# A block-sparse attention and a bilinear layer on one core: the second chunk's first-layer products are no longer parked in DRAM, and follow those of the first chunk

## The chip, the cores and the metric

One core of a Trainium2 chip. The metric is the device time of one execution in microseconds (us), lower is better. PE is the matrix engine, DVE the vector engine, ACT the scalar engine, POOL GpSimd, SP the engine whose queue issues most DMAs; ACT issues some too. PEld is PE's weight load.

## The reference, cut to what matters

```python
B, H, S, D = 4, 8, 768, 64                      # block of 32 positions, 24 blocks
scores = scale * q @ k^T                         # 768 x 768 for each of 32 heads
mask   = |blk_i - blk_j| <= 1, or first/last block row or column,
         or one of 3 sampled blocks of this query block
attn   = softmax(where(mask, scores, -1e9)) @ v
x      = attn.transpose(0, 2, 1, 3).reshape(3072, 512)
out    = ((x @ w_a) * (x @ w_b)) @ w_out         # 512 -> 1536 -> 512, fp32
```

## The kernel before

Work is cut into 12 **chunks** of 256 positions (3 in each of 4 batches) and each chunk into 8 **units**, one block of 32 query positions over all 8 heads; unit number n counts in the order of the work, so chunk 0 is units 0 to 7, chunk 1 units 8 to 15, chunk 2 units 16 to 23. Units whose block is the first or last of a batch are dense (units 8, 23, 24, ...), the others gather 8 key blocks.

*Attention of a unit* (`attend`, `attend_quad`): scores `s` on PE, row minimum `low` on DVE, exponentials `sm` on ACT (L898, L990), both 16-bit halves `hl` on ACT or DVE (L790, L793, L797), a transposing DMA `pt<-hl` on SP's queue (L920, L1015), and products `av` with the gathered values `VG` on PE (L816). Two units share one `av` tile; `output_half` writes its two halves as `xT` (L1060, L1063), the input of the layer. `s` has 2 buffers, `sm`, `hl` and `pt` 3 each. In `values` ACT also reads each block of raw values from `stage` (`va`, L515); the loads that fill `stage` are issued from ACT's own queue (L472, L507).

*The layer of a chunk cc* is 12 pieces f of 128 columns. First products `ab` (L1098, 24 matmuls): x times piece f of `w_a` and `w_b`; 2 buffers. `inner` makes the product `a` on ACT and DVE (L1126, L1129; 3 buffers of tag "a"), `split` its two parts `gh` (ACT, L1153) and `gl` (DVE, L1156; 2 buffers each). Second products `o` (L1184 to L1186, 6 matmuls): both parts times piece f of `w_out`, summed over f in two PSUM banks, which the next chunk may use when `store` has copied them (L1199, L1200). The weights come in and are prepared on the run while chunk 0 is worked on.

What is special in this kernel is **chunk 1**. Its first products stand in a flow of their own beside those of chunk 0 and wait for the same weights (`w_ready[f]`). Its products `a` are not split: `inner` writes each to DRAM (`parked_g`, L1134, 128 KB), and when the second products of chunk 1 begin, `unpark` reads them back as `u` (L1147) and splits these. Chunk 2's first products wait until all of it is split (`split_done`).

The order of all instructions is made when the kernel is built. Every piece of work is a flow (a Python generator) that asks for an engine; `Plan.run` gives the engine to the request that could start first by the planner's estimates, weighed with a rank (units have the lowest, `R_P2` second products, `R_P1` first products). Within an engine the program then runs in just this order: what waits holds up what stands behind it. This goes for SP's and ACT's DMA queues too.

Of the kernel before, what the change touches and what calls it, by code (L numbers as in the profile page):

```python
# [11 lines left out]
F32 = mybir.dt.float32  # L12
# [23 lines left out]
A_BUFS = 3  # L36
# [16 lines left out]
LEAD_K, LEAD_V, LEAD_Q, LEAD_X, LEAD_G = 10, 9, 8, -1, 2  # L53
GATE_KV, GATE_Q, GATE_G = 10, 5, 4
R_W, R_W_STEP = 8, 0.2
PARK = True
W_PE, W_DVE, W_ACT, W_POOL, W_SP = 0, 1, 0, 0, 2
SLACK = 0
R_NOW, R_P2, R_P1 = -50, 8000, 9000
# [179 lines left out]
def sp(ns, moved, fn):  # L239
    return [Way("SP", ns, fn, moved)]  # L240
# [3 lines left out]
def kernel(  # L244
# [40 lines left out]
    def take(tag, bufs):  # L285
        return rings.setdefault(tag, Ring(bufs)).take()
# [782 lines left out]
            read.fire(left.at + LATE_AV)  # L1069


    parked_g = dram.tile([NF, P, CH], F32, name="parked_g")
    g_parked = [Event() for _ in range(NF)]
    split_done = [Event() for _ in range(NF)]
    ready = {(cc, f): Event() for cc in range(NC) for f in range(NF)}
    parts = {}
    f1_ready = {(b, f): Event() for b in range(B) for f in range(NF)}

    def first_products(ccs):
        for cc in ccs:  # L1080
            b, c = chunks[cc]
            xc = xT[cc % 2]
            yield x_ready[cc]
            if cc == 2 and PARK:
                yield split_done[NF - 1]
            if cc == 0:
                plan.start(second_products(), R_P2)
            for f in range(NF):
                if cc < 2 and (cc == 0 or PARK):
                    yield w_ready[f]  # L1090
                read = yield from take("ab", 2)
                ab = psum.tile([P, 2, CH], F32, tag="ab", name=f"ab{cc}_{f}", bufs=2)

                def products(f=f):
                    for i in range(2):
                        for kt in range(KT):
                            for part, a in ((0, 0), (1, 0), (0, 1)):
                                mm(  # L1098
                                    ab[:, i, :], wab[:, f, i, part, kt, :], xc[:, kt, a, :],
                                    start=(i == 0 and kt == 0 and part + a == 0),  # L1100
                                    stop=(kt == KT - 1 and a == 1),
                                    skip_group_check=True,
                                )

                t = yield pe(2680, products)
                if f == NF - 1:
                    ffn_done[cc].fire(t)
                plan.start(inner(cc, f, ab, read), R_NOW, t)

    def inner(cc, f, ab, read):  # L1110
        b, c = chunks[cc]
        fb = f1[b % 2]
        fs = slice(0, NF) if b > 0 else slice(f, f + 1)
        rb = rscale[:, at_v + b : at_v + b + 1]
        if cc % NCH == 0 and (b == 0 or f == 0):
            pair = rscale[:, at_w + 2 * fs.start : at_w + 2 * fs.stop]
            pair = pair.rearrange("p (f i) -> p f i", i=2)
            t = yield dve(220, lambda: nc.vector.scalar_tensor_tensor(
                fb[:, fs], pair[:, :, 0], rb, pair[:, :, 1], ALU.mult, ALU.mult
            ))  # L1120
            f1_ready[b, f].fire(t)
        else:
            yield f1_ready[b, f if b == 0 else 0]
        e_a = yield from take("a", A_BUFS)
        a_sb = work.tile([P, CH], F32, tag="a", name=f"a{cc}_{f}", bufs=A_BUFS)
        yield act(470, lambda: nc.scalar.activation(  # L1126
            a_sb, ab[:, 0, :], AF.Copy, scale=fb[:, f : f + 1]
        ))
        t = yield dve(420, lambda: nc.vector.scalar_tensor_tensor(  # L1129
            a_sb, a_sb, rb, ab[:, 1, :], ALU.mult, ALU.mult  # L1130
        ))
        read.fire(t)
        if cc == 1 and PARK:
            t = yield sp(650, 364, lambda: nc.sync.dma_start(parked_g[f], a_sb))  # L1134
            e_a.fire(t)
            g_parked[f].fire(t)
            return
        yield from split(cc, f, a_sb, e_a)

    def unpark():  # L1140
        for f in range(NF):
            yield g_parked[f]
            if f >= 2:
                yield split_done[f - 2]
            e_a = yield from take("a", A_BUFS)
            a_sb = work.tile([P, CH], F32, tag="a", name=f"u{f}", bufs=A_BUFS)
            t = yield sp(650, 364, lambda f=f: nc.sync.dma_start(a_sb, parked_g[f]))  # L1147
            plan.start(split(1, f, a_sb, e_a), R_NOW, t)

    def split(cc, f, a_sb, e_a):  # L1150
        e_h = yield from take("gh", 2)
# [5 lines left out]
        e_a.fire(t)  # L1157
        parts[cc, f] = (gh, gl, e_h, e_l)
        ready[cc, f].fire(t + LATE_G)
        if cc == 1 and PARK:  # L1160
            split_done[f].fire(t)

    def second_products():
        banks, o_read = [None] * NJ, [None] * NJ
        for cc in range(NC):
            b, c = chunks[cc]
            if cc == 1 and PARK:
                plan.start(unpark(), R_NOW)
            rows = out[b * S + c * CH : b * S + (c + 1) * CH, :].rearrange(
                "(j p) d -> j p d", j=NJ  # L1170
            )
# [35 lines left out]
    with tc.manual_schedule():  # L1207
# [8 lines left out]
        plan.start(gather_keys(0), -LEAD_G)  # L1216
        plan.start(gather_values(0), -LEAD_G)
        plan.start(attend(*units[0]), 0)
        if PARK:
            plan.start(first_products([0, *range(2, NC)]), R_P1)  # L1220
            plan.start(first_products([1]), R_P1 + 1)
        else:
            plan.start(first_products(range(NC)), R_P1)
        plan.run()


# [64 lines left out]
```

## Time and profile before

| what | value |
|---|---|
| device time, median of 3 runs (range) | 901.85 us (900.5 to 905.66) |
| the profiled execution: its own time / its span | 901.24 us / 899.5 us |
| busy in the span: PE, PEld, DVE, ACT, POOL | 86%, 69%, 64%, 52%, 20% |

The span is what the profiler saw between the first and the last instruction; 1.7 us lie around it. A busy share is a mean over the whole span. "Granted clock" is the TensorE clock as a share of its full 2.4 GHz; 0.5 is its other level, 1.2 GHz.

### The profile page before, as it was taken

The numbers are of one execution on the slowest core, as the hardware profiler recorded it, in microseconds if no ns is written. First come the engines' busy times: TensorE is split into PE (matmuls) and PEld (weight loads), VectorE is DVE, ScalarE is ACT, GpSimd is POOL, SyncE is SP. The second block draws the span as 40 slices with busy tenths as digits, with TensorE's granted clock in tenths as the row PEclk, the third lists the DMA queues.
The fourth block names the chain that finished last, engine by engine and source line by source line (L and its number), as shares of the span: only waits on it lengthen the run. The fifth ranks groups of instructions, "written<-read, shape, count | busy, mean of one in ns | idle before, by whom it ended". The sixth has DMA issues, their size and how long they took to land.

```text
span 899.5 us, 23840 instructions
## 1 busy us (share of the span) xinstructions
PE 770.2 (86%) x9024; PEld 619.3 (69%) x9024; DVE 580.0 (64%) x1533; ACT 464.3 (52%) x1118; POOL 176.9 (20%) x416
## 2 busy tenths in 40 slices
PE   0132499678989999999999899999998999999998
PEld 0022277557768777777777678788776878888886
DVE  3898999986558677665677577645867736342222
ACT  4675576586446566754456468335536424232222
POOL 0652142322003332110132331001322200000000
PEclk9998599899999999999999999999999999999999
DMA  9978999979878699985867999637766516351000
GB/s 228 287 186 218 243 235 252 222 193 206 215 205 181 140 194 210 198 181 136 173 155 170 180 211 206 153 82 159 180 134 155 125 29 153 80 121 27 25 1 24
DMA packets 212221, 145.50 MB, mean 162 GB/s; under 512 B 152841, under 2 KB 180490, under 8 KB 211338
## 3 DMA queue, kind: packets, MB, share of 16 engines
q1 hardware_dynamic: 201280, 106.22, 54.3%
q10 hardware_dynamic: 10826, 37.76, 14.4%
q8 instruction: 71, 1.16, 0.5%
q14 instruction: 44, 0.36, 0.1%
HBM read 87.82 MB, written 14.16 MB: 113 GB/s over the span
## 4 chain that ended last, share of the span: by engine, by line
PE 55%; DMA 14%; DVE 10%; ACT 7%; issue 2%; SPq 2%; ACTq 0%; POOL 0%
PE ab L1098 30%; PE o L1184 6%; PE av L816 5%; DMA pt<-hl 5%; PE o L1186 5%; PE o L1185 5%; DMA q<-in_q_dram 3%; PE s L772 3%; DVE low L888 1%; DVE hl L797 1%; DVE xT L1063 1%; DMA VG<-vd 1%; DVE QT L649 1%; DMA u<-parked_g 1%; ACT sm L898 1%
## 5 line engine op out<-in xcount | busy, mean ns | idle before, releaser
L1098 PE MATMUL ab<-xT,wab 128*128 128x256 f16 x3456 | 404.7, 274 | 12.7 <-ACT xT L1060 6.9
L1098 PEld LDWEIGHTS <-wab 128*128 128x128 f16 x3456 | 329.7, 98 | 78.5 <-issue 37.7
L1129 DVE SCALAR_TENSOR_TENSOR a<-a,rscale,ab 128x256 f32<-128x256 f32 x144 | 68.6, 478 | 112.1 <-ACT a L1126 110.9
L1184 PE MATMUL o<-woh,gh 128*128 128x512 f32 x288 | 127.1, 441 | 6.8 <-ACT gh L1153 6.4
L1126 ACT ACTIVATE a<-ab,f 128x256 f32<-128x256 f32 x144 | 67.5, 468 | 120.3 <-PE ab L1098 114.4
L898 ACT ACTIVATE sm<-s,low,cq 128x256 f32<-128x256 f32 x176 | 97.9, 559 | 58.7 <-DVE low L891 29.4
L816 PE MATMUL av<-pt,VG 128*128 128x64 f16 x2688 | 103.2, 196 | 28.9 <-DMA pt<-hl 14.9
L816 PEld LDWEIGHTS <-VG 128*128 128x128 f16 x2688 | 94.6, 100 | 48.1 <-issue 35.5
L573 POOL COPY KG<-keysT 128x384 int32<-128x384 int32 x88 | 56.9, 647 | 356.5 <-PE s L772 325.9
L797 DVE SCALAR_TENSOR_TENSOR hl<-sm,den,hl 128x256 f16<-128x256 f32 (+1 forms) x208 | 104.3, 510 | 21.4 <-ACT hl L790 18.6
L1186 PE MATMUL o<-woh,gl 128*128 128x512 f32 x288 | 115.2, 400 | 0.5 <-DVE gl L1156 0.5
L1185 PE MATMUL o<-wol,gh 128*128 128x512 f32 x288 | 113.6, 395 | 0.0
L578 POOL COPY KG<-keysT 128x128 int32 x264 | 94.5, 394 | 42.9 <-POOL KG L573 23.2
L1153 ACT CAST gh<-a 128x256 fp32r<-128x256 f32 x132 | 53.1, 403 | 59.2 <-DVE a L1129 58.0
L1156 DVE TENSOR_TENSOR gl<-a,gh 128x256 fp32r<-128x256 f32 x132 | 58.2, 441 | 32.3 <-ACT gh L1153 31.6
L1184 PEld LDWEIGHTS o<-woh,gh 128*128 128x128 f32 x288 | 54.7, 190 | 27.7 <-ACT gh L1153 10.0
L772 PE MATMUL s<-KG,QT 128*32 128x256 f16 x1408 | 58.8, 291 | 16.8 <-DMA QT<-QT 16.6
L873 PE MATMUL s<-mrows,ident 128*32 128x192 bf16 (+1 forms) x352 | 25.6, 280 | 54.7 <-ACT sm L898 27.8
L1063 DVE SCALAR_TENSOR_TENSOR xT<-av,xT 64x256 f16<-64x256 f32 x96 | 40.4, 421 | 44.3 <-ACT xT L1060 43.4
L1186 PEld LDWEIGHTS o<-woh,gl 128*128 128x128 f32 x288 | 54.6, 189 | 16.6 <-DVE gl L1156 4.3
L888 DVE TENSOR_REDUCE low<-s 128x2 f32<-128x512 f32 x88 | 59.9, 682 | 6.4 <-PE s L772 6.1
L772 PEld LDWEIGHTS <-QT 128*32 128x32 f16 x1664 | 43.7, 101 | 29.5 <-issue 24.1
(92 smaller groups left out, 736.0 us busy)
## 6 DMA issues: line engine op xcount, KB each, us to landing
VG<-vd SPq DMA_DIRECT2D x284, 64.0 KB, 2.2
VG<-vd SPq DMA_DIRECT2D x88, 192.0 KB, 3.3
VG<-vd SPq DMA_DIRECT2D x32, 384.0 KB, 3.8
q<-in_q_dram ACTq DMA_DIRECT2D x12, 512.0 KB, 6.0
QT<-QT SPq DMA_DIRECT2D x24, 256.0 KB, 3.8
vd<-vs SPq DMA_DIRECT2D x16, 384.0 KB, 4.1
out_dram<-ou SPq DMA_DIRECT2D x24, 256.0 KB, 2.4
stage<-in_k_dram ACTq DMA_DIRECT2D x12, 384.0 KB, 4.2
```

The costliest lines, as they stand in the source:

```text
L578: nc.gpsimd.tensor_copy(to[:, :, (5 + r) * w : (6 + r) * w], of[:, :, bass.ds(at, w)])
L772: mm(to[h * BLK : (h + 1) * BLK], q_block(cc, i, 4 * hq + h, a), rhs(4 * hq + h), start=(first and a == 0), stop=(a == 1), skip_group_chec ...
L797: t = yield dve(221 + n * 1.03, lambda: nc.vector.scalar_tensor_tensor(lo, sm, over, hi, ALU.mult, ALU.subtract))
L816: mm(av[:, g, i % 2, :], w, pt[:, y, cols], start=(i % 2 == 0 and g == 0 and first and n + m == 0), stop=(last and n == len(terms) - 1 and ...
L888: yield dve(685, lambda: nc.vector.tensor_reduce(mx, ps, axis=mybir.AxisListType.X, op=ALU.max, negate=True))
L898: t = yield act(750, lambda hq=hq: nc.scalar.activation(sm[:, hq], ps[:, hq], AF.Exp, bias=low[:, at, hq, 0:1], scale=cq[:, cc, hq : hq + ...
L1098: mm(ab[:, i, :], wab[:, f, i, part, kt, :], xc[:, kt, a, :], start=(i == 0 and kt == 0 and part + a == 0), stop=(kt == KT - 1 and a == 1) ...
L1126: yield act(470, lambda: nc.scalar.activation(a_sb, ab[:, 0, :], AF.Copy, scale=fb[:, f : f + 1]))
L1129: t = yield dve(420, lambda: nc.vector.scalar_tensor_tensor(a_sb, a_sb, rb, ab[:, 1, :], ALU.mult, ALU.mult))
L1184: mm(po, gh[:, js], woh[:, f, :], start=(f == 0), stop=False)
L1185: mm(po, gh[:, js], wol[:, f, :], start=False, stop=False)
L1186: mm(po, gl[:, js], woh[:, f, :], start=False, stop=(f == NF - 1))
```

## The change

Chunk 1 is treated like all others: its first products wait in one flow behind those of chunk 0, its products are split as they are made, and `parked_g`, `unpark`, `split_done` and the 24 transfers are gone.

```diff
-    def first_products(ccs):
-        for cc in ccs:
+    def first_products():
+        for cc in range(NC):
             b, c = chunks[cc]
             xc = xT[cc % 2]
             yield x_ready[cc]
-            if cc == 2 and PARK:
-                yield split_done[NF - 1]
             if cc == 0:
                 plan.start(second_products(), R_P2)
             for f in range(NF):
-                if cc < 2 and (cc == 0 or PARK):
+                if cc == 0:
                     yield w_ready[f]
...
         read.fire(t)
-        if cc == 1 and PARK:
-            t = yield sp(650, 364, lambda: nc.sync.dma_start(parked_g[f], a_sb))
-            e_a.fire(t)
-            g_parked[f].fire(t)
-            return
         yield from split(cc, f, a_sb, e_a)
-
-    def unpark():
-        for f in range(NF):
-            yield g_parked[f]
-            if f >= 2:
-                yield split_done[f - 2]
-            e_a = yield from take("a", A_BUFS)
-            a_sb = work.tile([P, CH], F32, tag="a", name=f"u{f}", bufs=A_BUFS)
-            t = yield sp(650, 364, lambda f=f: nc.sync.dma_start(a_sb, parked_g[f]))
-            plan.start(split(1, f, a_sb, e_a), R_NOW, t)
...
         for cc in range(NC):
             b, c = chunks[cc]
-            if cc == 1 and PARK:
-                plan.start(unpark(), R_NOW)
...
-        if PARK:
-            plan.start(first_products([0, *range(2, NC)]), R_P1)
-            plan.start(first_products([1]), R_P1 + 1)
-        else:
-            plan.start(first_products(range(NC)), R_P1)
+        plan.start(first_products(), R_P1)
         plan.run()
```

Since the planner makes the order anew, instructions move. Ahead of the places shown here, which the trace before reaches at 202 us (SP, and ACT and DVE with the split of f = 0) and 207.69 us (PE), the order is the same on every engine. Line numbers of the changed kernel are 1 lower up to L1060 and 6 to 25 lower in the layer.

SP's queue, from the transposing load of the third block of keys of batch 1 (`keysT1<-ks1_2`) on: `pt17` and `pt18` are the transposed rows of units 17 and 18, `ou0_0` and `ou0_1` the output of chunk 0. Before:

```order
L496 DMA_TRANSPOSE keysT1_78<-ks1_2_2571 128x12x128
L1134 DMA parked_g_103<-a1_0_2720 128x256
L1134 DMA parked_g_103<-a1_1_2784 128x256
L673 DMA QT3_2468<-QT3_2468 64x2048 x2
L920 DMA_TRANSPOSE pt17_2566<-hl17_2515 128x8x128
L1147 DMA u0_2852<-parked_g_103 128x256
L1203 DMA out_0_dram<-ou0_0_2849 128x512
L1203 DMA out_0_dram<-ou0_1_2850 128x512
L1134 DMA parked_g_103<-a1_2_2884 128x256
L496 DMA_TRANSPOSE keysT1_78<-ks1_3_2679 128x12x128
L1147 DMA u1_2927<-parked_g_103 128x256
L920 DMA_TRANSPOSE pt18_2814<-hl18_2756 128x8x128
```

The same place of SP's queue in the changed kernel:

```order
L495 DMA_TRANSPOSE keysT1_78<-ks1_2_2570 128x12x128
L672 DMA QT3_2467<-QT3_2467 64x2048 x2
L919 DMA_TRANSPOSE pt17_2565<-hl17_2514 128x8x128
L1178 DMA out_0_dram<-ou0_0_2848 128x512
L1178 DMA out_0_dram<-ou0_1_2849 128x512
L919 DMA_TRANSPOSE pt18_2815<-hl18_2755 128x8x128
L495 DMA_TRANSPOSE keysT1_78<-ks1_3_2678 128x12x128
L919 DMA_TRANSPOSE pt19_2839<-hl19_2785 128x8x128
```

Two parkings no longer stand ahead of `pt17`, and `pt18` comes right behind the output stores, ahead of the last block of keys.

ACT, from the product `a1_2` (chunk 1, f = 2) on: `sm21` and `sm22` are exponentials of units 21 and 22, `va1_3` the reading of a raw value block of batch 1. Before:

```order
L1126 ACTIVATE a1_2_2884<-ab1_2_2804,f1_0_97 128x256
L898 ACTIVATE sm21_2887,den_96<-s21_2753,low_95,cq_94 128x256
L898 ACTIVATE sm22_2959,den_96<-s22_2889,low_95,cq_94 128x256 x2
L515 ACTIVATE va1_3_2901,bound_v_90<-stage_76 128x768
L1153 CAST gh1_0_2926<-u0_2852 128x256
L1126 ACTIVATE a1_3_3004<-ab1_3_2885,f1_0_97 128x256
```

The same place of ACT in the changed kernel:

```order
L1120 ACTIVATE a1_2_2887<-ab1_2_2804,f1_0_97 128x256
L897 ACTIVATE sm21_2862,den_96<-s21_2752,low_95,cq_94 128x256 x2
L506 DMA stage_76<-in_v_dram 128x768
L897 ACTIVATE sm22_2945,den_96<-s22_2860,low_95,cq_94 128x256
L1132 CAST gh1_2_2937<-a1_2_2887 128x256
L897 ACTIVATE sm22_2945,den_96<-s22_2860,low_95,cq_94 128x256
L514 ACTIVATE va1_3_2943,bound_v_90<-stage_76 128x768
L1120 ACTIVATE a1_3_2989<-ab1_3_2888,f1_0_97 128x256
L1059 ACTIVATE xT0_87<-av0_16_2549 64x4x64 x2
L1132 CAST gh1_3_3038<-a1_3_2989 128x256
```

The load that fills the buffer which `va1_3` reads is now issued behind both exponentials of unit 21 (before, it stood ahead of `a1_2`), and the split of f = 0 to 2 stands ahead of `va1_3` where before the first one, of `u0`, stood behind it.

On PE the same rows stand at this place in another order. Before, behind the scores of unit 22: `ab1_3`, `ab1_4`, `av` of unit 17, scores of unit 23, and only then `o` of f = 0. In the changed kernel: `o` of f = 0 and 1, `ab1_3`, `av` of unit 17, the first half of the scores of unit 23, `av` of unit 18, the second half, `o` of f = 2 and 3, `ab1_4`. Further on, before, `ab2_0` (the first product of chunk 2) follows the last `av` of unit 23 directly; in the changed kernel the scores of unit 27 and an `av` of unit 24 stand between, and `o` of f = 11 comes behind `ab2_0`. PE's order is the same in both again from the eleventh first product of chunk 6 on.

## Rows read from the trace of the kernel before

**Rows 1.** The page: busy us of the engines (share of the span) and instructions, and PE's busy tenths in 40 equal slices of the span (22.5 us each).
```profile
PE 770.2 (86%) x9024; PEld 619.3 (69%) x9024; DVE 580.0 (64%) x1533; ACT 464.3 (52%) x1118; POOL 176.9 (20%) x416
...
PE   0132499678989999999999899999998999999998
```

**Rows 2.** Busy time by stage: from us : to us, length, busy us (instructions) of PE, PEld, DVE, ACT, POOL, granted clock, share of the DMA engines' time, GB/s.
```profile
211.00:272.00 61.00, 54.50 (x604) 42.43 (x601) 35.08 (x90) 28.79 (x71) 7.62 (x21) 0.97 0.83 206
272.00:580.00 308.00, 296.02 (x3734) 238.10 (x3733) 214.80 (x595) 180.94 (x443) 73.10 (x192) 1.00 0.83 179
580.00:900.00 320.00, 309.96 (x3307) 253.35 (x3303) 152.33 (x400) 118.76 (x298) 30.68 (x82) 1.00 0.40 93
```

**Rows 3.** PE's waits between 272 and 580 us, the three largest of seven groups: instruction waited <- what ended the wait: us in all, times, longest.
```profile
PE av L816 <- DMA pt<-hl: 3.4, 2, 2.6
PE s L873 <- ACT sm L898: 3.3, 4, 1.3
PE o L1184 <- ACT gh L1153: 3.2, 5, 1.4
```

**Rows 4.** PE in order of time, the rows with a wait between 207 and 272 us, and the row where the order begins to differ: start, us, what, [idle before <- what ended it].
```profile
207.69 5.42 PE L1098 MATMUL ab<-xT,wab 128*128 128x256 f16 x48
215.05 0.88 PE L816 MATMUL av<-pt,VG 128*128 128x64 f16 x24 [1.95 <-DMA pt<-hl]
218.77 2.78 PE L1098 MATMUL ab<-xT,wab 128*128 128x256 f16 x24 [0.44 <-DVE a L1129]
259.27 0.69 PE L816 MATMUL av<-pt,VG 128*128 128x64 f16 x18 [0.22 <-DMA pt<-hl]
262.35 0.79 PE L1184 MATMUL o<-woh,gh 128*128 128x512 f32 x1 [2.39 <-ACT gh L1153]
268.75 0.38 PE L1098 MATMUL ab<-xT,wab 128*128 128x256 f16 x2 [0.85 <-ACT xT L1060]
269.65 2.56 PE L1098 MATMUL ab<-xT,wab 128*128 128x256 f16 x22 [0.52 <-DVE xT L1063]
```

**Rows 5.** PE in order of time, pieces of work that follow each other without a wait at full clock; the distance of two starts is what a piece takes.
```profile
241.57 0.47 PE L1184 MATMUL o<-woh,gh 128*128 128x512 f32 x1
...
243.04 2.79 PE L1098 MATMUL ab<-xT,wab 128*128 128x256 f16 x24
245.67 0.86 PE L816 MATMUL av<-pt,VG 128*128 128x64 f16 x24
246.47 0.51 PE L772 MATMUL s<-keysT,QT 128*32 128x384 f16 x8
246.91 0.87 PE L816 MATMUL av<-pt,VG 128*128 128x64 f16 x24
```

**Rows 6.** The granted clock in the 2 us in which the wait until 262.35 ends (columns as in rows 2), and PE's rows of 18 `av` matmuls, each with the row behind it, once before and once after that wait.
```profile
262.00:264.00 2.00, 1.65 (x4) 1.37 (x5) 1.04 (x2) 1.91 (x5) 0.00 (x0) 0.53 0.98 172
...
257.59 0.70 PE L816 MATMUL av<-pt,VG 128*128 128x64 f16 x18
258.22 0.83 PE L772 MATMUL s<-keysT,QT 128*32 128x384 f16 x16
...
265.08 0.90 PE L816 MATMUL av<-pt,VG 128*128 128x64 f16 x18
265.91 0.40 PE L873 MATMUL s<-mrows,ident 128*32 128x512 bf16 x4
```

**Rows 7.** SP's queue in order of time from the loads of keys on: start, us of issuing, what.
```profile
202.24 2.84 SPq L1134 DMA_DIRECT2D parked_g<-a  x2
205.13 1.13 SPq L673 DMA_DIRECT2D QT<-QT  x2
206.30 2.27 SPq L920 DMA_TRANSPOSE pt<-hl  x1
...
209.94 1.71 SPq L1203 DMA_DIRECT2D out_dram<-ou  x2
...
216.13 2.00 SPq L920 DMA_TRANSPOSE pt<-hl  x1
```

**Rows 8.** DVE and ACT in order of time, where they waited for a transfer: two of DVE for a buffer of `hl`, then ACT's issue of a load of values, and its wait for it.
```profile
215.04 0.35 DVE L793 TENSOR_SCALAR hl<-sm,den 128x256 f16<-128x256 f32 x1 [5.05 <-DMA pt<-hl]
243.77 0.42 DVE L793 TENSOR_SCALAR hl<-sm,den 128x384 f16<-128x384 f32 x1 [2.94 <-DMA pt<-hl]
...
207.49 0.33 ACTq L507 DMA_DIRECT2D stage<-in_v_dram  x1
214.73 0.84 ACT L515 ACTIVATE va<-stage 128x768 f16<-128x768 f32 x1 [3.53 <-DMA stage<-in_v_dram]
```

**Rows 9.** The transfers: first all between 202 and 260 us and two kinds of them (KB each, median us from issue to landing); then who waited for `u`; then us to landing, smallest, median and largest, of `pt` (200 to 262 us) and of the value loads (190 to 225 us).
```profile
DMA packets 20977, 12.02 MB, mean 207 GB/s; under 512 B 12702, under 2 KB 19514, under 8 KB 20969
...
parked_g<-a SPq DMA_DIRECT2D x12, 128.0 KB, 2.0
u<-parked_g SPq DMA_DIRECT2D x12, 128.0 KB, 3.1
...
  ACT gh L1153: 16.8, 9
...
DMA to landing us min/median/max: 3.2/4.0/8.7
...
DMA to landing us min/median/max: 3.5/3.9/7.2
```

More of the change, by code (lines that the diff above doesn't have):

```diff
@@ L55 @@
 R_W, R_W_STEP = 8, 0.2
-PARK = True
 W_PE, W_DVE, W_ACT, W_POOL, W_SP = 0, 1, 0, 0, 2
@@ L1069, in output_half @@
             read.fire(left.at + LATE_AV)
-    parked_g = dram.tile([NF, P, CH], F32, name="parked_g")
-    g_parked = [Event() for _ in range(NF)]
-    split_done = [Event() for _ in range(NF)]
     ready = {(cc, f): Event() for cc in range(NC) for f in range(NF)}
@@ L1159, in split @@
         ready[cc, f].fire(t + LATE_G)
-        if cc == 1 and PARK:
-            split_done[f].fire(t)
     def second_products():
@@ L1166, in second_products @@
             b, c = chunks[cc]
-            if cc == 1 and PARK:
-                plan.start(unpark(), R_NOW)
             rows = out[b * S + c * CH : b * S + (c + 1) * CH, :].rearrange(
```

## The prediction

> **What bounds the kernel now.** I read the page's head first, then the busy time by stage, then PE's waits, and last the queues of the one minute stretch in which the two kernels differ most. The head shows PE busy 770 of 899.5 us, and the slices show where it is not: in the first seven or so, while weights come in; from then on each slice is 8 or 9 tenths busy [rows 1]. The stages say the same in us: from 272 to 580 us PE is idle 12.0 of 308, from 580 to 900 10.0 of 320, but from 211 to 272 us 6.5 of 61, and there alone the granted clock is below 1 [rows 2]. From the place where the orders part, then, PE's work plus its waits is the time. The change adds and takes away no matmul; what it can move is PE's waits behind 207.69 us, where PE starts `ab1_3` and `ab1_4` in one run of 48 [rows 4] and the changed order puts second products first. All that lies ahead of this is the same work, in the same order but for a few splits of f = 0 and 1 on ACT and DVE, and I take its time over.
>
> **What it gives back.** In the stretch of chunk 1 PE waits six times [rows 4]: 1.95 (the `av` of unit 17 for its transposed rows `pt17`), 0.44, 0.22, 2.39 (the last second product of the chunk, for the last product fetched back), and 0.85 and 0.52 (the first product of chunk 2, for `xT` of unit 23). Sum 6.37 us. With the wait of 2.39 the granted clock falls to 0.53 in those 2 us, for the most part its lower level of 1.2 GHz [rows 6]. What this costs is read from pieces on both sides: a group of six second products takes 243.04 - 241.57 = 1.47 us at full clock [rows 5], but from 262.35 to 265.08, 2.73 us, in the slow piece [rows 4, 6]; 18 `av` matmuls take 0.63 before and 0.83 behind [rows 6]. 1.26 + 0.20 = 1.46 us. Together 7.83 us that need not come again.
>
> By the Trainium skill, "TensorE: Matmul & The Clock Gate", section "What's actually happening", the array's slow state is the default and activity lifts it. The trace agrees, since the clock is low only behind the longest of these waits; by that rule a new wait of the like would cost its 1.46 us over again, which the bounds below hold.
>
> **What it puts in their place.** I walk along the changed order with the durations of before: group of second products 1.47, first products 2.63, `av` of a unit 0.80, half of a dense unit's scores 0.44 [rows 5].
>
> (i) *`pt17`.* SP loses two parkings ahead of it, 2.84 us of issuing (some of it waiting for the product) [rows 7]. So it lands at 215.05 - 2.84 = 212.2. PE comes to its `av` at 207.69 + 2 x 1.47 + 2.63 = 213.3: no wait, 1.1 us in hand. If the parkings had held up nothing it would be 1.8.
>
> (ii) *`pt18`.* Issued at 216.13 before [rows 7]. Now it stands behind `QT`, `pt17` and the two output stores: 202.3 + 1.13 + 2.27 = 205.7, then the stores, which wait for DVE's copy (about 207) and take 1.71: 208.7. Landing takes 4.0 (median) to 8.7 (largest) [rows 9]: 212.7 to 217.4. PE needs it at 213.3 + 0.80 + 0.44 = 214.5. Wait 0 to 2.9. I take 0, since the 8.7 is `pt17` itself in the queue that loses the parkings.
>
> (iii) *`a1_3`.* ACT issued the last value load at 207.49 and waited 3.53 us until it had landed [rows 8]. The load now stands behind two splits `gh`, the product `a1_2` and both exponentials of unit 21, about 2.6 us more: 210.1. It lands 3.9 (median) to 7.2 us (this very one) later [rows 9]: 214.0 to 217.3. Behind `va1_3` on ACT stand `a1_3`, two `xT` and `gh1_3`; with DVE's part `gl1_3` is ready some 3 us later, 217.0 to 220.3. PE comes to it at 214.5 + 0.80 + 0.44 + 1.47 = 217.2. Wait 0 to 3.1, nearer the median because the load on the DMA engines falls: the 24 transfers of 128 KB are 3.1 of the 12.0 MB moved from 202 to 260 us [rows 9]. I take 0.7.
>
> (iv) *`xT` of unit 23.* PE waited 0.85 + 0.52 = 1.37 for it [rows 4]. Scores of unit 27 (about the 0.44 of half a dense unit) and 18 `av` matmuls (0.63) now stand between, 1.07. Left: 0.3; bound 1.37, as before.
>
> (v) *The split of the last product* no longer waits for a transfer. Between first and second products of f = 11 lie `ab2_0` and attention, 5 us and more, for a chain of four short operations: 0.
>
> (vi) *The rest of the stretch* I can't walk instruction by instruction. The nearest rows are those of chunks that are not parked: 12.0 us of waits in 308 us behind 272 [rows 2], 0.039 per us, or 2.4 us for these 61 us. The walk gives 0.7 + 0.3 = 1.0. I take 2.4 for everything, as the row counts what a walk overlooks. Bounds: 0, if all margins hold; and, as waits in a row of one engine cover each other, 3.1 (ii with iii) + 1.37 + 2.6 (the longest wait for a `pt` behind 272 [rows 3]) + 1.46 of clock = 8.5.
>
> Cost at nothing: the 24 issues gone from SP. They were hidden from PE except as said: ACT waited 16.8 us for `u` in nine waits [rows 9], of which 2.39 reached PE. Their room in DRAM and in the buffers "a" was cover as well: before, PE could run first products ahead of the second. If that cover is missed, the price is the third rival below.
>
> Behind 272 us the order differs up to the end of chunk 6, but of the same kinds of work: 12.0 us of waits in 272 to 580, of which I expect as much again. Three groups make up 9.9 of them, the longest 2.6 [rows 3]; if a third of it goes or comes, it is 4 us either way, which goes into the range. Behind, the order is the same.
>
> **Sum.** 901.24 (the profiled execution: span 899.5 and 1.74 around it) - 6.37 - 1.46 + 2.4 = 895.8. The profiled execution is 0.6 below the median of 901.85, so the gain against the median would be 6.0 us, 0.67%. About 0.5%, 4.5 us, is what the measurement can tell from no change; 897.3 is that line. By the bounds of the stretch alone the time is 893.4 to 901.9.
>
> **Rivals.** *PE's work decides, and nothing measurable changes.* Each wait taken away comes again in another place, since second products now stand close behind their first products. For it: PE's 770 us stay as they are, ACT's 16.8 us of waiting for `u` shrank to 2.39 on PE, and the chunks behind 272 have such waits without any parking: 3.2 us for `gh`, 3.4 for `pt` [rows 3]. Against: in those chunks they come to 0.039 per us, not to the 0.107 of this stretch. With all 7.83 coming again: 901.2. It decides if new waits are between 3.3 and 12.3 us. By the Trainium skill, "Perfetto Trace Analysis", section "Identifying Performance Opportunities", gains come from the most-contended engine; that would be this case, for PE loses no instruction.
>
> *Slower: the queues of DVE and ACT reach PE directly.* DVE stood 5.05 and 2.94 us for a free `hl` buffer, with products of the layer queued behind [rows 8]; PE felt 0.44 of it, since it had first products to run ahead with. Now `o` of f = 2 and 3 stand ahead of `ab1_4`. If both waits reach PE in full, with (iii) at 3.1 and another stretch at the low clock: 7.99 + 3.1 + 1.46 = 12.6 in place of 7.83, 906.0. Against: both were waits for transposes that SP issued late, and SP loses just the work ahead of them. It decides from new waits of 12.3 us on.
>
> *More than forecast:* no new wait at all, and the attention of units 21 to 24, which gets its transposes 3 to 7 us earlier, spares a third of the waits behind 272: 889.4.
>
> **How the numbers follow.** The forecast, 893 to 899, holds 0.5; no measurable change, around 901, 0.33; slower, around 906, 0.1; more than forecast, around 890, 0.07. Predicted 895.8. The range goes from 891 (the bound 893.4 with part of the 4 us) to 903 (the bound 901.9 with a little of it), and leaves out some 2 in 10: half of the slower case, some of the case of no change above 903, and the lowest. Past the line of 0.5% lie the case below and about nine tenths of the forecast, which I put down to 0.51 in all for the unsure 4 us; within it 0.39; slower 0.10.
>
> **What would show it.** Right: no wait above 1 us at the `av` of unit 17; granted clock 1.00 all the way from 202 us to the end; the first matmul of chunk 2's first products at about 264 us, not 268.75 (its end at 272.14 - 7.83 + 2.4 - 0.2); waits from there to 580 near 12 us. Wrong: a wait of PE for `gl` or `gh` near 217 to 221 us above 3, behind ACT's `va1_3`; a second spell of half clock; waits behind 272 that grew by as much as the stretch gave.

## The result: slower by 0.7%, and the profile after

The changed kernel took 912.12 us (median of 20 runs, 901.57 to 916.51); the kernel before, run beside it, 903.25 (20 runs, 895.84 to 910.68). The ratio is 1.0072, 95% interval 1.0048 to 1.0096: slower, where 895.8 was forecast. (Here and below, ratios leave out every execution more than 1.5% above the fastest of its kernel, and medians count them all, one of 2,702 us among them.) The profiled execution took 909.98 us, its span 908.2.

The page's head and the busy time by stage, columns as in [rows 1] and [rows 2]:

```profile
PE 778.1 (86%) x9024; PEld 625.8 (69%) x9024; DVE 579.9 (64%) x1537; ACT 464.0 (51%) x1114; POOL 176.1 (19%) x416
```

```profile
211.00:272.00 61.00, 58.53 (x714) 47.12 (x713) 35.67 (x95) 27.21 (x67) 10.48 (x29) 0.97 0.76 151
272.00:580.00 308.00, 288.12 (x3544) 231.60 (x3542) 206.48 (x575) 178.76 (x433) 72.14 (x184) 0.97 0.80 174
580.00:900.00 320.00, 313.66 (x3372) 257.01 (x3370) 155.88 (x411) 120.60 (x302) 30.77 (x82) 1.00 0.42 95
...
216.00:221.00 5.00, 4.59 (x40) 3.42 (x40) 4.46 (x11) 3.58 (x9) 2.17 (x8) 0.66 0.78 196
...
272.00:286.00 14.00, 6.26 (x78) 4.31 (x76) 8.13 (x24) 8.67 (x18) 1.83 (x6) 0.63 0.91 163
```

PE's matmuls are the same 9,024. PE is busy 7.9 us longer, of which 3.5 lie in the first 207.7 us, where PE's order is still the same, and 2.3 in the stretch of low clock described below. From 211 to 272 us PE idles 2.5 us where it idled 6.5 [rows 2], as forecast. From 272 to 580 us it idles 19.9 us where it idled 12.0, and the clock falls there. Nearly all of the difference lies in 14 us, 272 to 286: PE is busy for 6.26 of them, at a mean granted clock of 0.63, where the kernel before is busy for all 14 at 1.00.

The transfers between 202 and 260 us, 12.02 MB before [rows 9], are 1.76 MB less, and not the 3.1 MB of the parking, since PE is ahead and more value loads and transposes fall into these 58 us:

```profile
DMA packets 20160, 10.26 MB, mean 177 GB/s; under 512 B 13884, under 2 KB 18737, under 8 KB 20152
```

PE in order of time, the rows of chunk 1 and of the start of chunk 2, columns as in [rows 4]:

```profile
212.90 0.86 PE L815 MATMUL av<-pt,VG 128*128 128x64 f16 x24
213.69 0.51 PE L771 MATMUL s<-keysT,QT 128*32 128x384 f16 x8
216.41 1.34 PE L815 MATMUL av<-pt,VG 128*128 128x64 f16 x24 [2.21 <-DMA pt<-hl]
217.68 0.83 PE L771 MATMUL s<-keysT,QT 128*32 128x384 f16 x8
218.44 0.80 PE L1159 MATMUL o<-woh,gh 128*128 128x512 f32 x1
...
263.64 0.38 PE L1092 MATMUL ab<-xT,wab 128*128 128x256 f16 x2
264.29 2.56 PE L1092 MATMUL ab<-xT,wab 128*128 128x256 f16 x22 [0.27 <-DVE xT L1062]
277.39 1.14 PE L815 MATMUL av<-pt,VG 128*128 128x64 f16 x18 [5.06 <-DMA VG<-vd]
281.21 0.35 PE L872 MATMUL s<-mrows,ident 128*32 128x192 bf16 x4 [2.68 <-ACT sm L897]
```

The first product of chunk 2 starts at 263.64 us (before 268.75 [rows 4]): PE is 5.1 us ahead. From 272.33 us on, nine us later, it stands for 5.06 us, and then for 2.68. What it waits for is seen on the queues. First SP, then ACT's queue and ACT itself, then DVE, in order of time (start, us, what, [idle before <- what ended it]):

```profile
262.57 0.37 SPq L599 DMA_DIRECT2D VG<-vd  x1
263.04 2.28 SPq L1014 DMA_TRANSPOSE pt<-hl  x1
265.42 0.53 SPq L599 DMA_DIRECT2D VG<-vd  x1
268.01 1.22 SPq L1014 DMA_TRANSPOSE pt<-hl  x1
...
263.08 0.49 ACTq L633 DMA_DIRECT2D q<-in_q_dram  x1
...
276.89 0.51 ACT L789 ACTIVATE hl<-sm,den 128x256 f16<-128x256 f32 x1 [11.87 <-DMA pt<-hl]
277.31 0.46 ACT L1120 ACTIVATE a<-ab,f 128x256 f32<-128x256 f32 x1
...
277.80 0.48 DVE L1123 SCALAR_TENSOR_TENSOR a<-a,rscale,ab 128x256 f32<-128x256 f32 x1 [9.81 <-ACT a L1120]
```

ACT issues the load of the fifth chunk's queries (`q4`, 512 KB) at 263.08 us; SP issued the third transpose of attention unit 24 at 263.04. Before, `q4` went out at 272.25. Now see how long these transfers took, of the transfers issued from 262 to 278 us (KB each, median us from issue to landing), here and, below, in another execution of the same program (`changed_look6`, told of further down):

```profile
VG<-vd SPq DMA_DIRECT2D x3, 384.0 KB, 9.2
q<-in_q_dram ACTq DMA_DIRECT2D x1, 512.0 KB, 13.5
pt<-hl SPq DMA_TRANSPOSE x2, 11.9
```

```profile
VG<-vd SPq DMA_DIRECT2D x3, 384.0 KB, 5.5
q<-in_q_dram ACTq DMA_DIRECT2D x1, 512.0 KB, 7.9
pt<-hl SPq DMA_TRANSPOSE x3, 6.5
```

The load landed after 13.5 us; in the kernel before it took 5.6, and the transposes of its dense units 3.6 in the median and 6.6 at most. Single packets of 8 KB of the load took up to 5.5 us, against 0.9 at most before. Since `hl` has three buffers, ACT could not scale the rows of unit 26 until the transpose had read its one, and behind that scaling on ACT stood `a2_0` and the exponentials that PE waited for. I call this the crawl.

### The profile page after: what moved, and what is told of

It is laid out like the page before. It is cut to its first block, busy times and chain, and to the rows that moved or that the text cites. A ratio compares the mean times of both kernels' runs of the same rounds, so it can differ in the third digit from the quotient of the medians.

```text
span 908.2 us, 23776 instructions
## 1 busy us (share of the span) xinstructions
PE 778.1 (86%) x9024; PEld 625.8 (69%) x9024; DVE 579.9 (64%) x1537; ACT 464.0 (51%) x1114; POOL 176.1 (19%) x416
## 4 chain that ended last, share of the span: by engine, by line
PE 57%; DVE 12%; DMA 9%; ACT 5%; issue 4%; SPq 3%; POOL 0%; ACTq 0%; POOLq 0%
PE ab L1092 30%; PE o L1159 6%; PE av L815 6%; PE o L1161 5%; PE o L1160 5%; DMA pt<-hl 4%; PE s L771 3%; DVE hl L796 2%; DMA q<-in_q_dram 1%; DVE xT L1062 1%; DVE low L887 1%; DMA stage<-in_k_dram 1%; DVE a L1123 1%; DVE QT L648 1%; PE s L872 1%
## 5 line engine op out<-in xcount | busy, mean ns | idle before, releaser
L815 PEld LDWEIGHTS <-VG 128*128 128x128 f16 x2688 | 96.5, 101 | 46.3 <-issue 28.2
L1132 ACT CAST gh<-a 128x256 fp32r<-128x256 f32 x144 | 58.1, 403 | 69.1 <-DVE a L1123 66.4
L1135 DVE TENSOR_TENSOR gl<-a,gh 128x256 fp32r<-128x256 f32 x144 | 63.7, 442 | 27.6 <-ACT gh L1132 27.0
L792 DVE TENSOR_SCALAR hl<-sm,den 128x256 f16<-128x256 f32 (+1 forms) x123 | 43.9, 360 | 35.2 <-DMA pt<-hl 34.9
```

The costliest lines, as they stand in the source:

```text
L815: mm(av[:, g, i % 2, :], w, pt[:, y, cols], start=(i % 2 == 0 and g == 0 and first and n + m == 0), stop=(last and n == len(terms) - 1 and ...
L1135: t = yield dve(430, lambda: nc.vector.tensor_sub(gl, a_sb, gh.bitcast(F32)))
```

## The experiments

What I tested. Theory A: the crawl is the loss, and it comes from `q4` meeting a transpose, since the attention now runs 5 us earlier against ACT's loads. Theory B: the crawl is an accident of one execution, and the loss is spread over a redrawn order.

To compare executions I use the places at which both orders have done the same set of PE's matmuls: 1,360 of them (207.7 us before; from here the orders part), 2,050 (274.0, all of chunk 1 done), 2,372 (299.1), 3,448 (387.3), 5,878 (594.9, from here the orders agree) and all. For each profile the table has the time between two such places less that of the first profile of the kernel before, in us, worked out from the starts of PE's matmuls in the traces; "at 208" is how late PE comes to the first place.

```
                        q4 lands  at 208 | 208-274 274-299 299-387 387-595  to end |   sum
before                       5.6     0.0 |     0.0     0.0     0.0     0.0     0.0 |   0.0
before_look2                 5.2    +4.2 |    +0.1    +0.1    -1.5    +1.3    -0.1 |  -0.2
before_q4_early              5.9    +3.9 |    +0.1     0.0    +2.0    +2.0    -1.6 |  +2.6
before_q4_meet               5.6    +9.9 |    -2.8    +1.1    -0.8    +1.8    -2.2 |  -2.8
changed (the result)        13.5    -0.3 |    -4.7   +10.0    +2.0    +2.1    -0.3 |  +9.0
changed_again               14.0    +2.1 |    -7.7   +10.8    +6.1    +0.6    -1.2 |  +8.6
changed_look4               12.9    +0.2 |    -8.2    +8.8    +3.0    +0.7    -0.4 |  +4.0
changed_look5                9.3    +3.1 |    -8.6    +5.8    +5.5    +0.2    -0.9 |  +2.1
changed_look6                7.9    +2.5 |    -5.0    +4.4    -0.5    -0.6    +0.2 |  -1.5
changed_third                7.7   +12.5 |    -8.5    +4.1    +0.7    +2.7    -1.1 |  -2.1
changed_q4_late              5.5    +5.1 |    -4.7    +6.3    +0.4    +4.6    +0.2 |  +6.7
changed_q4_plus1             6.5    +9.4 |    -8.5    +0.9    +3.7    +1.1    +1.1 |  -1.8
changed_q4_on_sp             5.2    +6.1 |    -7.1    +0.8    +4.2    +0.7    +0.6 |  -0.9
changed_q4_early             4.7    +1.2 |    -8.6    -0.1    +8.2    +1.2    -0.8 |  -0.1
changed_q4_early_2           6.2    +3.6 |    -7.9    -0.1    +0.2    +2.1     0.0 |  -5.6
changed_q4_q6                5.2    +2.2 |    -7.4    -0.1    +4.6    +0.1    +2.2 |  -0.6
changed_q4_q6_2              4.8    +6.8 |    -8.6    +0.1    +1.4    +4.3    -0.7 |  -3.5
changed_q4_bytes             6.9    +2.5 |    -0.3    +1.1    +3.3    +1.9    -1.4 |  +4.6
```

And the medians in us, each with that of the kernel before on the same chip, and the ratio with its 95% interval:

```
changed_again       910.37  906.88  1.0003  0.9957 to 1.0050
changed_third       914.64  906.59  1.0136  1.0076 to 1.0196
changed_q4_late     908.30  906.88  1.0006  0.9963 to 1.0050
changed_q4_plus1    909.16  906.59  0.9990  0.9941 to 1.0040
changed_q4_on_sp    906.46  905.59  1.0005  0.9968 to 1.0043
changed_q4_early    904.17  906.88  0.9944  0.9903 to 0.9985
changed_q4_early_2  904.64  906.59  0.9985  0.9945 to 1.0026
changed_q4_q6       902.66  905.59  0.9988  0.9952 to 1.0025
changed_q4_q6_2     901.93  906.59  0.9958  0.9920 to 0.9996
changed_q4_bytes    908.25  905.59  1.0040  1.0006 to 1.0075
before_q4_early     906.06  906.88  0.9998  0.9960 to 1.0036
before_q4_meet      909.17  905.59  1.0034  0.9999 to 1.0069
```

**The unedited kernel again (no edit).**

> The changed kernel once more, nothing edited. Theory A (the load of the fifth chunk's queries, 512 KB on ACT's queue, meets the third DMA transpose of attention unit 24 in the same microseconds, and both crawl for 13 us): the order of issue on ACT and SP is fixed, so the meeting comes back. A profile again shows that load landing after 10 to 14 us and TensorE waiting 5 to 8 us between 272 and 285 us; ratio to the kernel before 1.005 to 1.010. Theory B (the crawl was an accident of that one execution, the loss is spread over many small waits): the load lands in 5 to 6 us, and the ratio is still 1.005 to 1.010.

> The changed kernel again, unedited, beside the next three on one chip. Theory A: the load of the fifth chunk's queries goes out within 0.1 us of unit 24's third transpose, as in both profiles so far (263.08 beside 263.04 us, 262.51 beside 262.46), and lands after 12 to 14 us; 3 to 8 us above the run with the load moved up. If the crawl is only sometimes there, the load lands in 5 to 8 us here.

> The changed kernel, one more profile. If the crawl is the loss: where the fifth chunk's load lands in over 10 us, TensorE's work from 202 us on takes 6 to 10 us more than in the kernel before; where it lands in 8 us or less, 0 to 3 us less than there. If the loss lies elsewhere, both kinds of profile show it.

> The same once more, same expectations as the profile ahead of it.

> The same once more, same expectations as the two profiles ahead of it.

In all six profiles the load goes out within 0.1 us of the third transpose of unit 24. It lands after 7.7 to 14.0 us, and the stretch from 274 to 299 us is longer than before by an amount that follows the landing: 4.1 at 7.7, 4.4 at 7.9, 5.8 at 9.3, 8.8 at 12.9, 10.0 at 13.5, 10.8 at 14.0. So the meeting always comes back, its price varies, and the sum of the execution goes with it: +9.0 and +8.6 us in the two slowest landings, -2.1 and -1.5 in the two fastest. The expectation that it lands in 10 to 14 us each time was too sharp, and the landings above 10 bring 4 to 9 us in the sum, not 6 to 10. `changed_third` has the fastest landing in its profile and the highest median; the executions that were only timed have no trace, so how often the crawl is strong in them is not known. Nor is the loss of the result found in every comparison: the ratio of `changed_again` is 1.0003 and its interval holds 1, where both theories had 1.005 to 1.010; that of `changed_third` is 1.0136.

**The kernel before again (no edit).**

> The kernel before, a second profile, for its own spread: the load of the fifth chunk's queries lands in 5 to 7 us again, and TensorE's work from 202 us on takes what it took in the first profile within 3 us, while the 200 us before that may differ by 5 to 10.

Landing 5.2 us, from 208 us on 0.2 us less than in the first profile: within what was expected.

**The load later on ACT, to where the kernel before has it.**

```diff
-        yield load_way(1400, lambda: nc.scalar.dma_start(t[:D], q[b, c]))
+        def load():
+            nc.scalar.dma_start(t[:D], q[b, c])
+
+        if cc == 4:
+            moved.append(load)
+        yield load_way(1400, (lambda: None) if cc == 4 else load)
...
             a_sb, ab[:, 0, :], AF.Copy, scale=fb[:, f : f + 1]
         ))
+        if (cc, f) == (2, 0):
+            moved.pop()()
```

> The changed kernel with one row of ACT's order moved: the load of the fifth chunk's queries is issued right behind the first-layer activation of chunk 2's first f, where the kernel before has it, and not ahead of the two scalings of units 25 and 26. All other rows on all engines stay. Theory A: the third and fourth transposes of unit 24 land in 3 to 5 us in place of 10 to 14, the 7.7 us of waits of TensorE at 277 and 281 us shrink to 3 or less, the half-clock spell of 10.2 us (worth some 5 us) goes; 8 to 12 us come back, 899 to 903 us, ratio to the kernel before 0.993 to 1.000. Theory B: the load was not the cause, the ratio stays 1.005 to 1.010.

908.30 us, only 2.1 below the unedited kernel on that chip: the crawl is gone (5.5 us), but the stretch still costs 6.3. Its own trace says why. ACT's and PE's rows:

```profile
273.94 0.49 ACTq L635 DMA_DIRECT2D q<-in_q_dram  x1
...
279.43 1.91 ACT L647 ACTIVATE QT<-q 64x2048 f16<-64x2048 f32 x1 [3.72 <-DMA q<-in_q_dram]
...
282.03 0.35 PE L878 MATMUL s<-mrows,ident 128*32 128x192 bf16 x4 [3.82 <-ACT sm L903]
```

ACT's reading of `q4` stands a few rows behind the load; it now waits for the landing, and PE for the exponentials behind it. A late load trades one wait for another; its time, 5 us above what theory A expected, doesn't tell A from B.

**The load one row later on ACT.** The edit is the one above, with the row issued behind the scaling of unit 25 (in `in_parts`) instead.

```diff
-            Way("ACT", 290 + n * 0.83, lambda: nc.scalar.activation(
+            Way("ACT", 290 + n * 0.83, lambda: (nc.scalar.activation(
                 hi, sm, AF.Copy, scale=over
-            )),
+            ), moved and moved.pop()())),
```

> The changed kernel with the fifth chunk's load one row later on ACT, behind the scaling of unit 25 (about 1.5 us later, 264.6 us), all else the same. If the crawl needs the load's packets in the second half of the transpose (its writes began 2 us behind its issue), 1.5 us more makes the load's packets come behind them: it lands in 5 to 7 us, the time is that of the run with the load moved up. If any overlap will do, it lands in 10 us or more and the time is as unmoved.

Here 1.5 us lie between the transpose and the load, and the landing is 6.5 us:

```profile
269.03 1.22 SPq L1020 DMA_TRANSPOSE pt<-hl  x1
270.34 1.79 SPq L599 DMA_DIRECT2D VG<-vd  x1
270.53 0.48 ACTq L635 DMA_DIRECT2D q<-in_q_dram  x1
```

The stretch costs 0.9 us, not 4 to 11; 909.16 us beside 914.64 for the unedited kernel on that chip, and the intervals of the two ratios (0.9990 and 1.0136) don't meet. One row of one queue is worth 5 us by the medians. The median is still 4.5 us above that of the run with the load moved up on this chip, where the same time was expected; the ratios of these two (0.9990 and 0.9985) agree.

**The load on SP's queue.**

```diff
-        yield load_way(1400, lambda: nc.scalar.dma_start(t[:D], q[b, c]))
+        by = nc.sync if cc == 4 else nc.scalar
+        yield load_way(1400, lambda: by.dma_start(t[:D], q[b, c]))
```

> The changed kernel with one row changed: the load of the fifth chunk's queries is issued by SP, in the queue that also carries the transposes and value loads, at the place that it had in the program's order, and not by ACT. Theory A, in its narrower form (the crawl needs two queues whose packets mix on the same DMA engines): in one queue the load goes behind the transpose ahead of it, lands in 5 to 8 us, and transposes land in 4 to 7; TensorE's waits at 272 to 285 us are 3 us or less, 900 to 905 us. If the crawl comes from the load being under way at the same time, whichever queue carries it, the load takes 10 us or more again and the time is as unmoved, ratio 1.003 to 1.008.

Landing 5.2 us, stretch 0.8, 906.46 us, 1.5 above the expected range. But SP issued the load only when the transpose was out, 2.7 us behind it (267.11 and 269.81 us), and the run ahead shows that 1.5 us are enough on ACT's queue too; in `changed_q4_late` the load stood 0.48 us behind a transpose and landed after 5.5. Whether two queues are needed for a crawl stays open.

**The load 35 us earlier.**

```diff
+    def load_q4():
+        t = work.tile([P, H, CH], F32, tag="rq", name="q4", bufs=1)
+        b, c = chunks[4]
+        nc.scalar.dma_start(t[:D], q[b, c])
+        moved.append(t)
...
         yield act(400, lambda: nc.scalar.copy(gh, a_sb))
+        if (cc, f) == (1, 5):
+            load_q4()
```

> The changed kernel with the same load moved the other way: issued behind the rounding of chunk 1's sixth f (some 20 us earlier, near 241 us, where neither a transpose nor a value load is under way). All other rows stay. Theory A: it lands in 4 to 6 us, unit 24's transposes in 3 to 5, and the time is as with the late load, 899 to 903 us, ratio 0.993 to 1.000. Theory B: 1.005 to 1.010, as unmoved.

> The kernel with the fifth chunk's load moved up to about 228 us, again, on the chip of the unedited one: 3 to 8 us below it, ratio to the kernel before 0.992 to 0.998.

It went out at 228.09 us (I had read the row's time wrongly when I wrote 241) and landed after 4.7. From 225 to 285 us, PE has one wait left (us in all, times, longest), where the unedited kernel adds 5.1 and 2.7 us to it:

```profile
PE ab L1102 <- DVE xT L1072: 0.3, 1, 0.3
```

The stretch from 274 to 299 us costs -0.1 in both profiles. On their chips the medians are 6.2 and 10.0 us below those of the unedited kernel, and 2.7 and 2.0 below the kernel before (904.17 and 904.64 us, where 899 to 903 was expected of the first). By the intervals the gain on the unedited kernel is clear on the second chip (0.9985 beside 1.0136) and not on the first (0.9944 beside 1.0003, intervals that overlap). One row of ACT's order takes the loss away, which theory A expects and B doesn't.

**That load and the seventh chunk's earlier.** `load_early(cc)` as above for both, at chunk 1's sixth and chunk 3's second f.

```diff
+    q_at = {4: (1, 5), 6: (3, 1)}
...
+        for n in q_at:
+            if q_at[n] == (cc, f):
+                load_early(n)
```

> The changed kernel with two loads moved up on ACT: the fifth chunk's queries as in the earlier run (behind the rounding of chunk 1's sixth f) and the seventh chunk's behind the rounding of chunk 3's second f (near 345 us instead of 359). All other rows stay. Theory: with the first crawl gone, part of the lead is given back between 320 and 385 us, where batch 2's keys and values are loaded; of that, the wait of ACT for the seventh chunk's load (3.15 us at 366.7) and of TensorE behind it (3.0 us at 369.8, and a half-clock spell of 3.4 us) goes: 3 to 5 us below the run with the one load moved, ratio to before 0.989 to 0.994. Rival: the stretch is paced by the transfers as a whole (their share is over 0.9 there), and another one is late instead: the same as with one load moved, 0.993 to 0.997.

> The kernel with the fifth and the seventh chunk's loads moved up, again: within 2 us of the run with the fifth's alone, since in the earlier profile the seventh's gave TensorE 3 us at 370 us and another wait took 1 to 2 back. If the seventh's load is worth what its wait was, 3 us below it.

902.66 and 901.93 us, 2.9 and 4.7 below the kernel before and the lowest medians of all; 2.7 below the run with one load moved on the chip that had both, between what the second expectation gives for either case. The first run's ratio, 0.9988, is above both ranges of its expectation. What the second load gives is not settled. By the intervals, one of two runs of either kernel is faster than the kernel before; the medians put them 0.2 to 0.5% below it.

**The transfers of the parking put back, unused** (with `q4` moved up, so without the crawl).

```diff
         read.fire(t)
+        if cc == 1:
+            nc.sync.dma_start(parked_g[f], a_sb)
         yield from split(cc, f, a_sb, e_a)
...
         parts[cc, f] = (gh, gl, e_h, e_l)
+        if cc == 1 and f > 0:
+            nc.sync.dma_start(parked_h[f - 1], parked_g[f - 1, 0:64])
```

> The changed kernel with the fifth chunk's load moved up as before, and the transfers of the parking put back without their use: SP writes each of chunk 1's twelve products to DRAM where it is made and copies half of the one before it from there to another place in DRAM (256 KB read and written for each, about what parking moves), and nothing waits for either but SP's own order. PE, DVE, POOL as in the changed kernel. If the gain between 202 and 272 us came from the transfers gone, TensorE waits for transposes of units 17 and 18 and value loads again (2 to 6 us more by 272 us) and the time is 3 to 7 us above the run with the load moved up. If it came from the order (products of chunk 1 between attention units instead of later ones), the time rises by 2 us or less.

908.25 us, and of the 7.4 to 8.6 us that the stretch of chunk 1 gives with `q4` moved up, 0.3 are left. PE's waits there:

```profile
224.99 0.77 PE L825 MATMUL av<-pt,VG 128*128 128x64 f16 x21 [1.00 <-DMA VG<-vd]
247.64 1.44 PE L825 MATMUL av<-pt,VG 128*128 128x64 f16 x24 [4.37 <-DMA pt<-hl]
```

PE's order is that of the changed kernel; no engine is seen to wait for the transfers, but SP stands 4.9 us in front of its writes from 204 to 250 us, until DVE releases them. So second products standing earlier don't give the 8 us by themselves: the 24 issues, SP's waits for them and their bytes must be gone from its queue. Which of the three counts is not told apart. (These are 23 issues, at other places than in the kernel before, and the copies are of 64 KB, so a product moves 192 KB where the parking moves 256; the 8 us are not the price of the parking.)

**The meeting provoked in the kernel before.** The same `load_q4`, issued behind the first exponential of unit 26, then behind the second of unit 25:

```diff
             ))
+            if (n, hq) == (25, 1):
+                load_q4()
         read.fire(t + LATE_S)
```

> The kernel before with the same load moved up two rows on ACT, between the two exponentials of unit 26 (near 271.0 instead of 272.25 us), so that its packets should start at 273 us, while the third transpose of unit 24 (issued at 271.03 us) still writes. All other rows stay. Theory A: the crawl shows up in a kernel that parks; the load lands in 9 to 14 us instead of 5.6, the transpose likewise, and the time rises by 3 to 10 us, ratio 1.003 to 1.010; if the packets miss the transpose's, no change. Theory B: no change, 0.998 to 1.002.

> The kernel before with the load of the fifth chunk's queries moved up four rows on ACT, behind the second exponential of unit 25, so that it is issued some 1 us ahead of the third transpose of unit 24 and not 1 us behind it. All other rows stay. Theory A: if the two meet within a few tenths of a us, the load lands in 9 to 14 us in this kernel too, TensorE waits 4 to 8 us at 275 to 285 us and the time rises by 4 to 10 us (ratio 1.004 to 1.011); if the load gets ahead of the transpose, it lands in 5 us and nothing changes (0.998 to 1.002).

The first missed: ACT was late, and the load went out 1.8 us behind the transpose and landed in 5.9; no change. The second met it to 0.02 us:

```profile
274.48 0.39 SPq L600 DMA_DIRECT2D VG<-vd  x1
276.01 1.47 SPq L1027 DMA_TRANSPOSE pt<-hl  x1
276.03 0.48 ACTq L631 DMA_DIRECT2D q<-in_q_dram  x1
...
DMA to landing us min/median/max: 7.0/7.4/7.8
```

The transposes landed after 7.0 and 7.8 us, the load after 5.6, and PE lost 1.1 us in the stretch: a meeting, but no crawl. 909.17 us is 3.6 above the kernel before with an interval that touches 1, and its profile shows no place where that was lost. So the crawl goes with the meeting (all six landings of `q4` above 7 us have it, and of the twelve others this one alone), but the meeting is not enough for it. One difference is in the traces: in all six profiles with the crawl SP issues a value load of 384 KB 0.47 us ahead of the transpose, as at 262.57 us in the result's, so that three transfers are issued within 0.51 us; here it went out 1.53 us ahead. No run moves that load alone, so whether it belongs to the crawl stays open.

## Why the prediction was wrong, by its own steps

**Chunk 1: right, and on the low side.** Forecast was 7.83 us back and 2.4 of new waits, net 5.4. Six profiles of the changed kernel give 4.7 to 8.6 from 208 to 274 us, mean 7.1. The steps below are those of the result's profile.

(i) `pt17`, no wait: right; `av` of unit 17 starts at 212.90 without one (213.3 in the walk). (ii) `pt18`, taken at 0 of a bound of 0 to 2.9: it was 2.21 us here, at 216.41. SP issued it at 207.42 (208.7 in the walk), and it landed after 8.9 us:

```profile
DMA to landing us min/median/max: 8.9/8.9/8.9
```

I had put the 8.7 of [rows 9] down to the parkings ahead of `pt17`; without them a transpose beside the value load (issued at 208.23) still took as long. The clock fell to 0.66 from 216 to 221 us, which I had only in the bounds: the group of second products behind it took 2.21 us (218.44 to 220.65) and not 1.47, the `av` 1.27 and not 0.80, 1.2 us together. This wait is 2.0 us in `changed_look6` as well, and 0.4 or less in the other four profiles, which are those that give 7.7 and more. (iii) No wait. (iv) 0.27, forecast 0.3. (v) No wait. (vi) All of 211 to 272 us: 2.48, forecast 2.4. The first product of chunk 2 came at 263.64, forecast 264.

**The step that failed: "behind 272 us ... 12.0 us of waits in 272 to 580, of which I expect as much again", 4 us either way.** It was 19.9, and some of the clock: two of the signs that the prediction named for being wrong, a second spell of half clock and waits behind 272 that grew by as much as the stretch gave. I took the stretch as one lump because its kinds of work stay. Two places made it wrong.

The first is the crawl, 274 to 299 us: 4.1 to 10.8 us, mean 7.3, as much as chunk 1 gives. In the result's profile it is 5.06 + 2.68 = 7.74 us of waits, and 2.3 of lower clock behind them. My second rival, *Slower*, had a mechanism of this kind (an engine stuck for an `hl` buffer with products of the layer behind it), but of DVE, and with its wait at 217 to 221 us; it came on ACT, 55 us later, by a load that I had not looked at, since its row in the kernel before costs nothing. The meeting was to be seen in advance: attention that comes 5 us earlier passes loads of ACT that other work sets off, and `q4` moved from behind `a2_0` to ahead of it. Its price was not: no load of queries whose landing the trace before shows took over 8.9 us.

The second is the stretch from 299 to 387 us, where batch 2's keys and values come in: mean +2.8 us in the unedited kernel, +3.7 with the crawl taken out, +/- 2 in the kernel before. PE's waits there, first three of seven in the kernel before (3.8 us in all), then the four of the changed one (5.1 us):

```profile
335.05 0.50 PE L1184 MATMUL o<-woh,gh 128*128 128x512 f32 x1 [1.39 <-ACT gh L1153]
342.00 0.27 PE L873 MATMUL s<-mrows,ident 128*32 128x192 bf16 x4 [1.00 <-ACT sm L898]
364.54 2.78 PE L1098 MATMUL ab<-xT,wab 128*128 128x256 f16 x24 [0.24 <-DVE a L1129]
```

```profile
336.30 0.62 PE L771 MATMUL s<-KG,QT 128*32 128x256 f16 x16 [0.63 <-DMA QT<-QT]
345.58 2.78 PE L1092 MATMUL ab<-xT,wab 128*128 128x256 f16 x24 [0.41 <-DVE a L1123]
353.72 0.50 PE L1159 MATMUL o<-woh,gh 128*128 128x512 f32 x1 [1.80 <-ACT ou L1174]
376.06 4.37 PE L1092 MATMUL ab<-xT,wab 128*128 128x256 f16 x24 [2.21 <-DVE a L1123]
```

The new order has waits of its own here, or longer ones: `QT` (0.6 to 2.3 us in the six profiles, 0.4 at most before), `ou` (0.8 to 2.8) and, in front of `ab` at 372 to 380 us, 1.4 to 4.4, some with a piece at the lower clock. With the seventh chunk's load moved up the last is gone in one profile (the stretch costs 4.6 all the same) and 2.0 in the other: what is late changes from run to run. I show these waits; which part of the new order makes each I did not take apart.

**The sum once more,** by the means of six profiles: -7.1 + 7.3 + 2.8 + 0.9 - 0.6 = +3.4 us, and with the crawl taken away -3.9. That this is near the forecast's -5.4 is in part luck: chunk 1 gives 1.7 more than forecast, and the rest of the order takes 3.1. The six profiles with the load out of the way (one row later, on SP, earlier) give -2.1 in the mean. So the crawl is the larger part of the loss, and the rest is spread over the redrawn order, as theory B had it. The medians of the unedited kernel are 8.9, 3.5 and 8.0 us above those of the kernel before, more than the 3.4 of its six profiles, which may be on the fast side.

## What to carry to other kernels

A change that moves one stream of work by a few us moves it past every queue that is not moved with it: list the large loads on other queues that get new neighbours, and look for one that now goes out with a DMA transpose. Behind the edit, "the same kinds of work" is not the same waits; a gain of 5 us needs either a walk over the next stretch too or a range that holds a loss of that size. And before a change is dropped, move the one row that it collides with: here that was worth 5 to 10 us by the medians, and the change itself, with the row moved, 2 to 5.

## What the runs showed of the hardware

- A plain load on one queue and a DMA transpose on the other, issued within 0.1 us, can slow each other far beyond their bytes: in 262 to 278 us of the result's profile 1.92 MB were moved, and the load took 7.7 to 14.0 us in six executions of one program, 4.7 to 6.9 with its row moved. It is not certain: the meeting provoked in the kernel before gave 5.6. Over the whole result's profile, 53 transposes of `hl` with no load of ACT seen under way took 3.4 us in the median and 6.3 at most; 19 beside one 5.4 and 13.8.
- By the Trainium skill, "DMA: Bandwidth & Descriptors", section "Issuing engines are not separate DMA queues", transfers of all engines run on the same 16 DMA engines and interleave. The trace agrees: from 262 to 278 us the packets of SP's queue took 69.7% and those of ACT's 31.8% of the engines' time, at 120 GB/s in all. By the Trainium skill, "DMA: Bandwidth & Descriptors", section "Rules for kernel authors", a transpose next to ordinary DMAs needs nothing, said where it tells how two transposes corrupt each other's data. Of time, the measurement says otherwise here.
- The first 208 us of one program differ by 13 us between executions: PE had done 1,360 matmuls from 0.3 us ahead of the first profile of the kernel before to 12.5 behind it, in six profiles of the unedited changed kernel. From there on, the two profiles of the unedited kernel before differ by 0.2 us in the sum, and by up to 1.5 in a stretch. A single execution can't show a change of 1% here; the time from a common place of PE's work leaves out that first part.
